# A block-recurrent attention and a bilinear feed-forward in one kernel: the output stage's products in another order, one unit's state copy on ScalarE, one unit's masks apart

## The chip, the cores and the metric

The kernel runs on one core of a Trainium2 chip. The core has five engines with a queue of instructions each. TensorE (PE) multiplies matrices; its weight loads are listed apart as PEld. VectorE (DVE) and ScalarE (ACT) read what PE has written to PSUM, and compute elementwise. GpSimd (POOL) computes elementwise between tiles in SBUF and starts transfers. SyncE (SP) starts transfers. Each engine works through its own queue in order and waits on semaphores for the others. The metric is the time of one execution in microseconds (us) on the device, smaller being better.

## The reference

Four batches of eight heads, 768 positions, 64 values per head. Attention goes through the sequence in blocks of 64: inside a block the scores are masked with a decaying lower triangle, and what came before enters through a 64x64 state per head.

```python
for b in range(nb):
    qb, kb, vb = (q[:, :, sl], k[:, :, sl], v[:, :, sl])
    intra = np.einsum('bhic,bhjc->bhij', qb, kb) * Dmask[None]
    intra = np.einsum('bhij,bhjd->bhid', intra, vb)
    inter = np.einsum('bhid,bhde->bhie', qb * lam_pow[None], kv_state)
    out[:, :, sl] = intra + inter
    kv_state = lam_block * kv_state + np.einsum('bhsd,bhse->bhde', kb_dec, vb)
...
a = x @ w_a          # x: the attention's output, 3072 x 512
b = x @ w_b          # 512 x 1536
return a * b @ w_out # 1536 x 512
```

## The kernel before

**Units and groups.** The 3072 rows are cut into 24 units of 128 rows (a batch has six), and these into seven groups of 4, 2, 4, 4, 4, 4 and 2 units (numbered 0 to 6). The attention works by unit and the feed-forward by group. While the feed-forward of one group runs on PE, pieces of attention for later units are put between its matmuls. Where they go is written out by hand in the table `PLAN`: for each group a list of (slot, piece, unit), and the function `hook(slot)` that the feed-forward calls at fixed points runs the pieces of that slot in the list's order. No planner decides anything at run time: each engine's queue is in the order in which the code issues.

**The pieces.** For unit u, `P` scales q and k by powers of lambda on POOL (L276), starts a transposing transfer on SP (L310) and loads v on POOL's queue (L298). `S` makes the scores: eight 64-row matmuls (L343) into two PSUM banks, then two masking multiplications on DVE into bf16 tiles (L360). `SA` and `SB` are the same cut in two: `SA` issues the matmuls and the first mask, `SB` the second mask (L463). `V` adds a unit to the state in a PSUM bank (L410) and copies it to SBUF: on DVE as one multiplication with a block-diagonal mask (L443), or, for the units in `ACT_COPY`, on ACT as two copies of 64 partitions (L441). `O2` makes the attention outputs of two units: the part from the state (64x64 matmuls) and the part from the masked scores (128x64 matmuls, both L379), which ACT copies to the group's input xT (L402). It then calls `sums` (L560 to L563): for the last unit of a group, four DVE additions that make the tile xs, sums of blocks of xT. It ends with the state matmuls of the second unit (L432), whose copy is made where the other copies are. `Q` is `O2` with one unit's scores beside it.

**The feed-forward** of groups 1 to 6 replaces eight block products with seven (`ffn_seven`). Products run into three kinds of banks, m_q, m_r and m_p (L582), in seven steps per slice of d_ff; ACT copies some banks out (L597: s, s5, u), DVE makes the sums c11 (L616, POOL L619 for some slices), c12 (L627) and c22 (L633) and the product ab (L636), and POOL makes the other half of ab (L629). Three links matter later. The last product of a slice runs into the bank that c22 is read from, so it waits for c22. c12 has two buffers, so the c12 of slice i+2 waits for POOL's ab of slice i. And product n = 3 waits for the copy s5, product n = 7 for the copy u.

**The output stage** of groups 2 to 5 (`out_seven`) does the same with the second matrix: products o_q, o_p, o_r (L693), each of twelve 256-column matmuls in groups of four units, from sums of blocks of ab, called sm, that DVE makes (`add_sums`; L730 makes the set with index 3, L732 the one with index 2). In group 5 an early branch is taken. In groups 2, 3 and 4 the tail issues, in order: o_q from set 1; slots 15 and 16 with the piece `O2`; half of o_r from set 3; o_q from set 2; the DVE addition L787 that reads o_q; the other half of o_r; the DVE addition L789 that reads o_r; the store of o1; slots 17 to 19, among them `G` (POOL waits for the tile xs, so that its next work doesn't start sooner), `P` twice or once, and `S` for the unit after; then a last o_q product into the bank that L787 has read, a copy by ACT (L795), and the store of o2. Stores and transposing transfers stand in the one queue of SP in this order.

**Banks.** PSUM has eight banks. One holds the state. The other seven are given out by `ps_bank`: the one that was used longest ago, among those not held.

Of the kernel before, what the change touches and what calls it, by code (L numbers as in the profile page):

```python
# [22 lines left out]
def _bc(ap, dims):  # L23
# [18 lines left out]
SUM_ON_VEC = {1: (2,), 2: (0, 1, 2, 3, 5), 3: range(6), 4: range(6), 5: (1, 2, 4, 5), 6: (0, 1, 2)}  # L42
O_SEVEN = (2, 3, 4, 5)
O_EARLY = (5,)
ACT_COPY = (4, 10, 12, 13, 14, 16, 17, 18, 20, 21)
FIRST_COPY = (11, 15, 19)
W_ORDER = ("a0", "a1", "b0", "b1", "a2", "b2", "a3", "b3", "a4", "a5", "b4", "b5", "o0", "q4", "k4", "o1", "v4",
           "q5", "k5", "o2", "v5", "o3")
# [14 lines left out]
}  # L63
for _g, _u in ((2, 10), (3, 14), (4, 18)):
    PLAN[_g] += [(11, "V", _u), (13, "Q", (_u, _u + 1, _u + 2)), (14, "V", _u + 2), (14, "S", _u + 3),
                 (16, "O2", (_u + 2, _u + 3)), (18, "S", _u + 4)]
PLAN[2] += [(_s, "W", None) for _s in (3, 3, 3, 4, 4, 4)]


# [1 line left out]
def kernel(  # L71
# [12 lines left out]
    B, H, S, D = q.shape  # L84
# [28 lines left out]
    bank = {"held": set(), "age": [0] * 7, "clock": 0}  # L113
# [155 lines left out]
    U = {}  # L269
# [59 lines left out]
    def score_banks():  # L329
        kq = Banks()  # L330
        kq.ids = []
        for i in range(2):
            kq.append(ps_bank(f"kq{i}", [128, HP, 128], F32))
            kq.ids.append(bank["last"])
        return kq

    def scores(u, kq=None):
        d = U[u]
        kq = kq or score_banks()
        for hp in range(HP):  # L340
            for i in range(2):
                p = slice(64 * i, 64 * i + 64)
                nc.tensor.matmul(kq[i][:, hp, :], lhsT=d["kT"][p, hp, :], rhs=d["qT"][p, hp, :],  # L343
                                 start=True, stop=True, skip_group_check=True)
        return kq

    def masks(u, kq):
        ms = mask(kq)
        U[u]["m"] = lambda i, hp: ms[i][:, hp, :]
# [99 lines left out]
    def piece_SA(u):  # L449
        kq = U[u]["kq"] = scores(u)  # L450
        U[u]["ms"] = [mask_one(kq, 0)]
        return [kq.ids[1]]

    def piece_SB(u):
        ms = U[u]["ms"]
        kq = U[u].pop("kq")
        ms.append(mask_one(kq, 1))
        U[u]["m"] = lambda i, hp: ms[i][:, hp, :]
        return [kq.ids[1]]
# [7 lines left out]
    def piece_V(u):  # L467
        kv_update(u)
        if u % NB < NB - 1:
            kv_copy(u, kv["ps"], "act" if u in ACT_COPY else "dve")  # L470

    xTs = {}

    def pieces_O(us, nxt=()):
        kqs = [score_banks() for u in nxt]
        o_banks(us)
        for u, kq in zip(nxt, kqs):
            scores(u, kq)
        for u in us:
            inter(u)  # L480
        for b in range(2):
            for u in us:
                intra(u, b)
            evac_o(us, b)
        sums(us[-1])
        beside = len(us) == 2 and us[0] >= n0 + 2
        if beside:
            kv_beside(us[1])
        copy = beside and us[1] % NB < NB - 1
        at = 0 if us[1] in FIRST_COPY else 1  # L490
        for n, (u, kq) in enumerate(zip(nxt, kqs)):
            if n == at and copy:
                kv_copy(us[1], kv["ps"])
            masks(u, kq)
        if copy and len(nxt) <= at:
            kv_copy(us[1], kv["ps"], "act" if us[1] in ACT_COPY else "dve")

# [54 lines left out]
    def sums(u):  # L552
        g = next(i for i in range(len(GROUPS)) if g_u0[i] <= u < g_u0[i] + GROUPS[i])
        if g not in S_GROUPS or u != g_u0[g] + GROUPS[g] - 1:
            return
        h = GROUPS[g] * BLK // 2
        x = xTs[u][0]
        t = wst_pool.tile([128, 4, 2, h], BF16, name="xs", tag="wst")
        x11, x12, x21, x22 = (x[:, k:k + 2, c:c + h] for c in (0, h) for k in (0, 2))
        nc.vector.tensor_add(t[:, 0], x22, x21)  # L560
        nc.vector.tensor_sub(t[:, 1], t[:, 0], x11)
        nc.vector.tensor_sub(t[:, 2], x11, x21)
        nc.vector.tensor_sub(t[:, 3], x12, t[:, 1])  # L563
        xs[g] = t
# [110 lines left out]
    def out_seven(u0, n, ab, hook, last_step, early):  # L675
        h, nt, js = n * BLK // 2, n // 2, range(FC // 4)
# [12 lines left out]
        def product(ps, x, w, js, first, ts=range(nt)):  # L689
            for t in ts:  # L690
                for j in js:
                    for c in range(2):
                        nc.tensor.matmul(ps[:, t, :], lhsT=x(j, c)[:, t * BLK:(t + 1) * BLK], rhs=w(j)[:, c, :],  # L693
                                         start=(first and t == 0 and j == js[0] and c == 0), stop=True,
                                         skip_group_check=True)
# [4 lines left out]
        def of_s(i):  # L700
            return lambda j, c: sm[i][j][:, c, :]

        def of_w(k, n):
            return lambda j: wo_block(j, k, n)
# [15 lines left out]
        def add_sums(js, which):  # L720
            for i in which:
                for j in js:
                    x22, x21, x11, x12 = xs4[j]
                    d = [sm[i][j] for i in range(4)]
                    if i == 0:
                        nc.vector.tensor_add(d[0], x22, x21)
                    elif i == 1:
                        nc.vector.tensor_sub(d[1], d[0], x11)
                    elif i == 3:
                        nc.vector.tensor_sub(d[3], x12, d[1])  # L730
                    else:
                        nc.vector.tensor_sub(d[2], x11, x21)  # L732
# [31 lines left out]
        r, rb = bank_of("o_r")  # L764
        product(r, of_s(0), of_t(0), js, True)
        s5 = snap("o_s5", "s5", r, 2)
        if not early:
            hook(FC + 2)
            add_sums(js, (3, 2))
        product(q, of_s(1), of_t(1), js, False)  # L770
        u2 = snap("o_u2", "c12", q, 2)
        if early:
# [9 lines left out]
            return  # L782
        hook(FC + 3)
        hook(FC + 4)
        product(r, of_s(3), of_w(1, 1), js, False, range(nt // 2))
        product(q, of_s(2), of_t(2), js, False)
        nc.vector.tensor_add(o2[:, :, 256:512], s5, q)  # L787
        product(r, of_s(3), of_w(1, 1), js, False, range(nt // 2, nt))
        nc.vector.tensor_add(o1[:, :, 256:512], u2, r)  # L789
        release(rb)  # L790
        put(u0, o1)
# [204 lines left out]
    for g, n in enumerate(GROUPS):  # L996
        if g + 1 < len(GROUPS):
            new_xT(g + 1)
        plan = {}
        for slot, name, us in PLAN.get(g, ()):  # L1000
            plan.setdefault(slot, []).append((name, us))

        def hook(slot, plan=plan):
            for name, us in plan.get(slot, ()):
                if name == "P":
                    prep_k(us)
                    if us in DMA_T:
                        make_vb(us)
                elif name == "QS":
                    make_qs(us, "pool")  # L1010
                elif name == "KS":
                    make_ks(us, "dve")
                    scaled(us)
                elif name == "LS":
                    wait_for(raw[us - 2, "k"])
                    load_x("q", us, nc.sync)
                    load_x("k", us, nc.sync)
                elif name == "L":
                    load_all(us)
                elif name == "TW":  # L1020
                    w_sums(us)
                elif name == "TO":
                    wo_sums(us)
                elif name == "G":
                    gate = singles.tile([1, 1], BF16, name="gate")
                    nc.gpsimd.tensor_copy(gate, xs[max(xs)][0:1, 3, 0, 0:1])
                elif name == "GT":
                    gate = singles.tile([1, 1], BF16, name="gate")
                    nc.gpsimd.tensor_copy(gate, two[max(two)][0:1, 3, 0, 0:1])
                elif name == "W":  # L1030
                    store_kept()
                elif name == "T":
                    piece_T(us)
                elif name == "SA":
                    bank["held"].update(piece_SA(us))
                elif name == "SB":
                    bank["held"].difference_update(piece_SB(us))
                elif name == "S":
                    piece_S(us)
                elif name == "V":  # L1040
                    piece_V(us)
                elif name == "O":
                    pieces_O((us,))
                elif name == "O2":
                    pieces_O(us)
                else:
                    pieces_O(us[:2], us[2:])

        if g in S_GROUPS:
            ffn_seven(g, g_u0[g], n, gx.pop(g), hook, g + 1 == len(GROUPS))  # L1050
        else:
            ffn(g_u0[g], n, gx.pop(g), hook, g == 0)
# [29 lines left out]
```

## Time and profile before

| | us |
|---|---|
| median of 9 runs | 218.79 |
| lowest, highest | 218.12, 221.62 |
| the profiled execution | 218.8 |
| its span in the profile | 217.1 |
| PE busy | 208.7 (96% of the span) |
| DVE busy | 175.3 (81%) |
| ACT busy | 106.6 (49%) |
| POOL busy | 124.7 (57%) |
| share of PE in the chain that ended last | 91% |

Busy times are the unions of the engine's instructions. The profiled execution took 1.7 us more than its span; that part lies before the first and behind the last recorded instruction. The granted clock of TensorE is at full speed in all slices. A timeline row gives start, length, engine, line, operation, tiles and count; a row of several matmuls ends, by the model for matmul ends, about 0.16 us after the next row may start, so the start of the next row is what counts. In square brackets stands how long the engine was idle before the row, and what released it.

### The profile page before, as it was taken

What the parts mean: (1) busy time and instruction counts of PE and PEld (TensorE: products, weight loads), DVE (VectorE), ACT (ScalarE), POOL (GpSimd) and SP (SyncE); (2) the same over time, 40 slices, a digit from 0 to 9 for tenths busy, and PEclk for the clock granted to TensorE, in tenths of its full rate; (3) what the DMA queues carried; (4) which work ended last, traced back from release to release, by engine and by line L of the source; (5) the groups of instructions that cost most, each with busy time, mean ns of one, the idle gap of its engine ahead of it and who ended that gap; (6) DMA issues with size and microseconds to landing.
All of it is one profiled execution on the core that took longest, in us unless ns stands there. A gap on an engine that the chain in (4) does not pass through costs nothing.

```text
span 217.1 us, 5765 instructions
## 1 busy us (share of the span) xinstructions
PE 208.7 (96%) x2323; PEld 161.9 (75%) x2331; DVE 175.3 (81%) x322; ACT 106.6 (49%) x195; POOL 124.7 (57%) x143
## 2 busy tenths in 40 slices
PE   7699999999899999999999999999999999999994
PEld 2376444555796688878888987888987888889973
DVE  0892899777878988999789999689999588996860
ACT  2586224256751565446465535555545556344522
POOL 5879659974679199820999310999310736300330
PEclk9999999999999999999999999999999999999999
DMA  4999999999999999990499990699900750002302
GB/s 125 301 177 188 196 230 215 224 217 188 132 196 171 159 168 264 242 226 13 126 190 190 227 145 3 144 174 230 138 0 3 151 118 0 3 2 78 118 3 97
DMA packets 86766, 31.31 MB, mean 144 GB/s; under 512 B 74068, under 2 KB 83156, under 8 KB 86740
## 3 DMA queue, kind: packets, MB, share of 16 engines
q1 hardware_dynamic: 53748, 20.39, 47.6%
q0 software_dynamic: 32704, 10.49, 43.0%
q8 instruction: 18, 0.29, 0.6%
q10 hardware_dynamic: 288, 0.07, 0.1%
q14 instruction: 8, 0.07, 0.1%
HBM read 28.32 MB, written 6.29 MB: 159 GB/s over the span
## 4 chain that ended last, share of the span: by engine, by line
PE 91%; DMA 3%; DVE 1%; SPq 1%; issue 1%; ACT 1%; ACTq 0%
PE m_q L582 24%; PE m_r L582 12%; PE op L819 10%; PE o_q L693 10%; PE m_p L582 6%; PE o_r L693 5%; PE o_ps L379 5%; PE b_ps L505 5%; PE a_ps L505 5%; PE kq L343 3%; DMA k<-in_k_dram 3%; PE o_p L693 2%; PE kvd L410 1%; SPq L229 1%; PE tps L321 1%
## 5 line engine op out<-in xcount | busy, mean ns | idle before, releaser
L629 POOL TENSOR_TENSOR ab<-c,c 128x512 bf16<-128x512 bf16 x30 | 34.9, 1168 | 33.5 <-DVE c L627 33.2
L582 PEld LDWEIGHTS <-tw 128*128 128x128 bf16 x576 | 48.7, 98 | 6.8 <-issue 1.3
L582 PE MATMUL m_q<-xs,tw 128*128 128x256 bf16 (+1 forms) x288 | 36.1, 255 | 0.1
L360 DVE TENSOR_TENSOR m<-kq,lotri 128x512 bf16<-128x512 f32 x41 | 25.8, 681 | 2.1 <-PE kq L343 2.1
L582 PEld LDWEIGHTS <-wa_sb 128*128 128x128 bf16 x288 | 24.7, 98 | 2.6
L597 ACT COPY s<-m_q 128x512 f32<-128x512 f32 x30 | 17.6, 588 | 17.8 <-PE m_q L582 17.6
L636 DVE TENSOR_TENSOR ab<-c,m_q 128x512 bf16<-128x512 f32 x30 | 20.5, 684 | 6.0 <-PE m_q L582 4.2
L627 DVE TENSOR_TENSOR c<-u,m_r 128x512 f32<-128x512 f32 x30 | 20.4, 681 | 3.7 <-ACT u L597 3.7
L298 POOL DMA_DIRECT2D vb<-in_v_dram x24 | 22.3, 932 | 1.3 <-DMA wo_sb<-in_moe_w_out_dram 1.2
L819 PE MATMUL op<-wo_sb,ab 128*128 128x512 bf16 (+2 forms) x114 | 22.1, 335 | 0.4 <-issue 0.2
L616 DVE TENSOR_TENSOR c<-s,m_p 128x512 bf16<-128x512 f32 x25 | 17.1, 685 | 6.7 <-PE m_p L582 5.8
L597 ACT COPY s<-m_r 128x512 f32<-128x512 f32 x30 | 17.7, 590 | 8.9 <-PE m_r L582 8.9
L597 ACT COPY u<-m_q 128x512 f32<-128x512 f32 x30 | 17.7, 591 | 7.2 <-PE m_q L582 5.9
L633 DVE TENSOR_TENSOR c<-s,m_q 128x512 f32<-128x512 f32 x30 | 20.5, 685 | 0.4
L693 PEld LDWEIGHTS <-sm 128*128 128x128 bf16 x192 | 17.5, 98 | 3.6 <-DVE sm L732 0.4
L276 POOL TENSOR_TENSOR qk<-qf,lp_q 128x512 bf16<-128x512 f32 x18 | 18.9, 1050 | 1.4 <-DMA qf<-in_q_dram 1.4
L582 PE MATMUL m_q<-xT,tw 128*128 128x256 bf16 (+1 forms) x144 | 18.1, 255 | 0.9 <-DVE c L633 0.9
L402 ACT CAST xT<-o_ps 128x512 bf16<-128x512 f32 x22 | 11.9, 588 | 12.9 <-PE o_ps L379 12.6
L582 PE MATMUL m_r<-xs,tw 128*128 128x256 bf16 (+1 forms) x144 | 18.1, 255 | 0.0
L582 PE MATMUL m_r<-xs,wb_sb 128*128 128x256 bf16 (+1 forms) x144 | 18.1, 255 | 0.0
L582 PE MATMUL m_q<-xT,wa_sb 128*128 128x256 bf16 (+1 forms) x144 | 18.1, 255 | 0.0
L582 PE MATMUL m_p<-xT,wa_sb 128*128 128x256 bf16 (+1 forms) x144 | 18.1, 255 | 0.0
(120 smaller groups left out, 362.3 us busy)
## 6 DMA issues: line engine op xcount, KB each, us to landing
out_dram<-o_two SPq DMA_DIRECT2D x8, 512.0 KB, 3.4
qf<-in_q_dram SPq DMA_DIRECT2D x14, 256.0 KB, 5.8
kf<-in_k_dram SPq DMA_DIRECT2D x14, 256.0 KB, 6.1
vb<-in_v_dram POOLq DMA_DIRECT2D x24, 128.0 KB, 5.9
wa_sb<-in_moe_w_a_dram POOLq DMA_DIRECT2D x6, 256.0 KB, 6.1
wb_sb<-in_moe_w_b_dram POOLq DMA_DIRECT2D x6, 256.0 KB, 7.5
wo_sb<-in_moe_w_out_dram POOLq DMA_DIRECT2D x6, 256.0 KB, 8.2
out_dram<-o_kept SPq DMA_DIRECT2D x6, 256.0 KB, 5.1
```

Source lines behind the costliest of these rows:

```text
L276: eng_of(eng).tensor_mul(dst.rearrange("p (c b) d -> p b c d", b=2), x[:].rearrange("p (b c) d -> p b c d", b=2), lp.rearrange("p (b c) o ...
L298: nc.gpsimd.dma_start(out=vb, in_=vr[b, nb])
L360: nc.vector.tensor_mul(m, kq[i], lotri_bc)
L505: nc.tensor.matmul(ps[:, lo:hi], lhsT=w_sb[:, s, f * 128:(f + 1) * 128], rhs=xT[:, s, lo:hi], start=(s == 0), stop=(s == KS - 1), skip_gro ...
L582: nc.tensor.matmul(ps[:, f, :], lhsT=w(k, f), rhs=x[:, k, :], start=(first and f == 0 and k == 0), stop=True, skip_group_check=True)
L597: nc.scalar.copy(t, ps)
L627: nc.vector.tensor_add(c12, d["u2"], d["r"])
L629: nc.gpsimd.tensor_mul(ab[:, nf * i:nf * i + nf, 0:h], d["c11"], c12)
L633: nc.vector.tensor_add(d["c22"], d["s5"], d["q"])
L636: nc.vector.tensor_mul(ab[:, nf * i:nf * i + nf, h:2 * h], d["c22"], d["q"])
L693: nc.tensor.matmul(ps[:, t, :], lhsT=x(j, c)[:, t * BLK:(t + 1) * BLK], rhs=w(j)[:, c, :], start=(first and t == 0 and j == js[0] and c == ...
L819: nc.tensor.matmul(op[:, lo:hi], lhsT=ab[:, f, t * 128:(t + 1) * 128], rhs=wo_sb[:, f, lo:hi], start=(f == 0), stop=(f == FC - 1))
```

## The change

Three things are changed, all in the order of issue or in the engine that does a piece. The arithmetic is the same, and so is the number of matmuls.

1. In the output stage of groups 2, 3 and 4, the piece `S` of slot 18 is cut in two: its score matmuls (`SK`) go to slot 16, ahead of the attention outputs, and its two masks (`SM`) to slot 17, behind `G` and `P`. Between `SK` and `SM` its two banks are held. The piece `O2` is called without its four sums (`OD`); they are issued later, behind L787. The two halves of o_r's product are joined and come behind o_q from set 2, and `add_sums` makes set 2 before set 3.
2. In group 1, the state copy of unit 6 moves from DVE to ACT.
3. In group 1, unit 7's scores and first mask are issued in slot 1 and its second mask in slot 2; the outputs of units 6 and 7 move from slot 4 to slot 5, between the scores and the masks of unit 8.

```diff
-ACT_COPY = (4, 10, 12, 13, 14, 16, 17, 18, 20, 21)
+ACT_COPY = (4, 6, 10, 12, 13, 14, 16, 17, 18, 20, 21)
...
-    1: [(0, "V", 6), (1, "S", 7), (4, "O2", (6, 7)), (4, "P", 10), (5, "S", 8),
+    1: [(0, "V", 6), (1, "SA", 7), (2, "SB", 7), (4, "P", 10), (5, "SK", 8), (5, "O2", (6, 7)), (5, "SM", 8),
         (6, "V", 8), (6, "P", 11), (7, "S", 9), (12, "O2", (8, 9))],
...
-                 (16, "O2", (_u + 2, _u + 3)), (18, "S", _u + 4)]
+                 (16, "SK", _u + 4), (16, "OD", (_u + 2, _u + 3)), (17, "SM", _u + 4)]
...
+    def piece_SK(u):
+        kq = U[u]["kq"] = scores(u)
+        return kq.ids
+
+    def piece_SM(u):
+        kq = U[u].pop("kq")
+        masks(u, kq)
+        return kq.ids
...
-    def pieces_O(us, nxt=()):
+    def pieces_O(us, nxt=(), defer=False):
...
-        sums(us[-1])
+        if defer:
+            late.append(us[-1])
+        else:
+            sums(us[-1])
...
-            add_sums(js, (3, 2))
+            add_sums(js, (2, 3))
...
-        product(r, of_s(3), of_w(1, 1), js, False, range(nt // 2))
         product(q, of_s(2), of_t(2), js, False)
         nc.vector.tensor_add(o2[:, :, 256:512], s5, q)
-        product(r, of_s(3), of_w(1, 1), js, False, range(nt // 2, nt))
+        while late:
+            sums(late.pop())
+        product(r, of_s(3), of_w(1, 1), js, False)
...
+                elif name == "SK":
+                    bank["held"].update(piece_SK(us))
+                elif name == "SM":
+                    bank["held"].difference_update(piece_SM(us))
+                elif name == "OD":
+                    pieces_O(us, defer=True)
```

More of the change, by code (lines that the diff above doesn't have):

```diff
@@ L470, in piece_V @@
             kv_copy(u, kv["ps"], "act" if u in ACT_COPY else "dve")
-    xTs = {}
-    def pieces_O(us, nxt=()):
+    xTs, late = {}, []
+    def pieces_O(us, nxt=(), defer=False):
         kqs = [score_banks() for u in nxt]
```

## The prediction, made before the changed kernel ran

> **What bounds the kernel now.** I read the engines' busy times and the summary of the chain that ended last first, then that chain inside group 1, then the timelines of PE and DVE in the output stage of group 3.
>
> ```profile
> PE 208.7 (96%) x2323; PEld 161.9 (75%) x2331; DVE 175.3 (81%) x322; ACT 106.6 (49%) x195; POOL 124.7 (57%) x143
> ...
> PE 91%; DMA 3%; DVE 1%; SPq 1%; issue 1%; ACT 1%; ACTq 0%
> ```
>
> PE sets the time nearly everywhere, so a change pays only where it shortens PE's own work or a wait of PE. The chain shows one stretch in group 1 where DVE leads:
>
> ```profile
> 55.93 0.57 PE m_r L582 x8
> ...
> 57.12 1.27 DVE m L360 x2
> 58.39 0.59 DVE c L627
> 58.99 0.61 DVE c L633
> 59.60 0.04 issue
> 59.64 0.61 PE m_q L582 x8
> ```
>
> The product at 59.64 waits for c22 (L633), and c22 stands in DVE's queue behind unit 6's state copy (56.52), unit 7's two masks (57.12) and c12. PE issued the product before at 58.11 and needs 0.45 for it, so it was ready at 58.56: 1.08 lost.
>
> PE, output stage of group 3:
>
> ```profile
> 130.59 1.49 PE L693 MATMUL o_q<-two,sm 128*128 128x256 bf16 x12
> 132.01 0.42 PE L379 MATMUL o_ps<-qkT,st 64*64 64x128 bf16 x16
> 132.36 0.64 PE L379 MATMUL o_ps<-m,vb 128*64 128x128 bf16 x16
> 132.93 0.83 PE L693 MATMUL o_r<-wo_sb,sm 128*128 128x256 bf16 x6
> 133.59 1.59 PE L693 MATMUL o_q<-two,sm 128*128 128x256 bf16 x12
> 135.02 0.82 PE L693 MATMUL o_r<-wo_sb,sm 128*128 128x256 bf16 x6
> 135.77 0.40 PE L343 MATMUL kq<-qkT 64*128 64x128 bf16 x8
> 136.19 1.47 PE L693 MATMUL o_q<-two,ab 128*128 128x256 bf16 x12
> 137.50 0.60 PE L582 MATMUL m_q<-xT,wa_sb 128*128 128x256 bf16 x4
> ```
>
> Read from start to start, twelve matmuls take 1.31 undisturbed (the last product) and six take 0.66 (132.93 to 133.59). Three rows are longer. DVE in the same stretch says why:
>
> ```profile
> 132.99 1.09 DVE L732 TENSOR_TENSOR sm<-ab 128x512 bf16<-128x512 bf16 x3
> 134.00 0.41 DVE L560 TENSOR_TENSOR xs<-xT 128x512 bf16<-128x512 bf16 x1
> ...
> 135.46 0.68 DVE L787 TENSOR_TENSOR o_two<-o_s,o_q 128x512 f32<-128x512 f32 x1
> 136.06 0.68 DVE L789 TENSOR_TENSOR o_two<-o_u,o_r 128x512 f32<-128x512 f32 x1
> ```
>
> The second o_q takes 1.43: its set 2 is finished only at 134.08. The second half of o_r takes 0.75: 0.09 is the switch from full matmuls to 64-row ones. The scores take 0.42 where 0.33 is usual (130.26 to 130.59): the last o_q must wait until L787 has read the bank, at 136.14.
>
> **The output stage, groups 2 to 4.** No matmul is added or removed. In group 3 the new order costs: o_q from set 1 with the switch 1.42, the scores 0.33, the state part of the outputs 0.35, the mask part 0.57 (all as above), then o_q, o_r and o_q at 1.31 each, 6.60 from 130.59 instead of 6.91: 0.31 saved. (Between scores and outputs nothing more is paid than the 0.33: at 127.25 and 127.58 of the trace the same sequence stands.) Group 2, 98.65 to 105.47, has 6.82 and comes to 1.42 + 0.33 + 0.93 + 3.93 = 6.61: 0.21. Group 4, 162.75 to 169.77, has 7.02 and comes to 1.41 + 0.33 + 1.04 + 3.93 = 6.71: 0.31. Together 0.83.
>
> Does a new wait take this back? In group 3, on the trace's clock: set 2 is now made first and ends at 133.08, and o_q from it begins at 133.26. Set 3 ends at 134.08, o_r begins at 134.57. L787 can start when o_q has ended, 134.83, and has read the bank at 135.5; the last o_q begins at 135.88. The scores come 3.7 earlier, and need their transposed q and k: unit 18's transfer starts at 121.13 and lands 6.7 later, at 127.8, for scores at 132.0. For units 14 and 22 it lands at 97.2 and 158.1, for scores at 100.1 and 164.2.
>
> What comes later is DVE. It idles from 134.08 to 134.83, then L787 until 135.43, the four sums 1.46 until 136.89, L789, and the two masks from 137.49 to 138.69, instead of 137.85. The next group's c11 is the next in that queue. It waits for m_p, which ends about 0.31 earlier than before, near 138.76: just covered (before, DVE idled 1.15 there). The second product of the group needs the first sum only, ready at 135.85. With the masks gone late, their banks are wanted by the next slice's m_r, at 140.86 before. L789's bank is wanted at 139.4. Both have a microsecond or more. So I book 0 here; without the cover each 0.1 of DVE would cost PE at most 0.1, through c12 and c22.
>
> [...] Two banks are now held through the outputs, beside o_q and o_r. Following the rule of `ps_bank`, the outputs get the banks of the second and third mask ahead of them in DVE's queue (in group 2: masks from 97.51 in steps of 0.61, the third read by 99.4; the outputs start at 100.4). By the row the price is 0; if pressure bit, with the banks of a mask not begun, it would be those 0.6 per mask, 1.8 over three groups. I take the row.
>
> POOL is moved too: `G` waits for the sums. Its copy goes from 103.58 to about 104.9 (+1.3) in group 2, and from 135.67 to 136.8 (+1.1) in group 3. Behind it wait the scalings, the v loads, SP's transposing transfers, the loads behind these, the store of o2, and POOL's ab. The one that meets PE: c12 of slice 4 waits for ab of slice 2. In group 3 that ab runs 117.75 to 118.9 and c12 starts at 120.80; after, 120.3 against 120.5. In group 4, 151.0 against 153.07 becomes 152.1 against 152.4. Margins of 0.2 and 0.3, so 0, but thin.
>
> **Group 1.** The copy leaves DVE (0.60 from start to start) and becomes two ACT copies. The rows of these have 0.37 each, 0.39 apart, so 0.78; the trace doesn't show another ACT copy right behind, so 0.64 (overlapped as the others are by 0.12 to 0.15) to 0.78. I take 0.78. [...] c22 doesn't depend on that much: DVE makes m0 at 56.52, c12 at 57.15 (u ends at 57.10), c22 from 57.80 to 58.48. PE, with product n = 7 at 57.15 and four more of 0.45, is ready at 58.94. No wait is left: 59.64 becomes 58.94, 0.70 gained.
>
> Most of it is lost again. The outputs of 6 and 7 now come behind unit 8's scores: one switch less (0.1), scores at 62.16, outputs at 62.5 (the second bank, of m_p, is read by c11 until 62.51: 0.08). The last state matmul starts at 63.37, and L443 for unit 7 follows 0.24 later, at 63.61. It now stands ahead of unit 8's masks, so the first starts at 64.21; before, at 64.32. From there DVE works without a gap in both orders: two masks, L636, c12, c22, the state copy of 8, two masks of 9, until 69.20. The outputs of 8 and 9 wait for the last mask: their last four matmuls started at 69.25. So PE arrives 0.6 early and waits; **0.11** is left. Group 2 follows with DVE full and PE full, both 0.11 earlier.
>
> **The sum**: 0.83 + 0.11 = 0.94. The profiled execution was 218.8 with a span of 217.1; the span becomes 216.2 and the time 217.9. The median of the runs, 218.79, is the same as the profiled one: **217.85**.
>
> **Rivals.**
> - A, *the gain of group 1 stays*: DVE has less behind it than I think, and PE keeps 0.6 to 0.8. For it: DVE idles 0.24 and 0.37 near 62 and 63 before. Against: its gapless row to 69.20. 218.79 - 0.83 - 0.7 = 217.25.
> - B, *slower*: POOL's late start becomes the wait. Place: c12 of slice 4 in groups 3 and 4. It decides from 0.2 and 0.3 beyond the delay worked out, and from there costs one for one. Were POOL one microsecond later still, because unit 18's k is loaded behind two delayed transposing transfers on SP (its scaling starts at 114.82, the load was issued at 108.21, and such loads take 6.1), it would cost 0.8 + 0.7: 219.35. Against: POOL found that k without a wait, and load and scaling are delayed alike.
> - C, *the waits only move*: the two short waits per output stage return at the head of the next group, where DVE has lost its 1.15 of slack, and only the switch (0.09 each) and little of group 1 stay: 218.45.
>
> **How the numbers follow.** Mine 0.55, with its own range 217.5 to 218.2; A 0.18, B 0.13, C 0.14. A measurement of this kernel tells about 0.2%, 0.44, from no change: faster below 218.35. Mine nearly wholly, A, and a quarter of C are faster, 0.75; the rest of C and a little of mine the same, 0.12; B slower, 0.13. The range 217.1 to 218.6 holds mine, most of A and most of C; B is left out.
>
> **What would show it.** In each output stage: o_q, o_r, o_q back to back at 1.31, and 6.6 to 6.7 from the second o_q to the next group. In group 1: no idle time ahead of the product that waits for c22, L443 of unit 7 near 63.6, and a new PE wait of about half a microsecond ahead of the outputs of 8 and 9. I am wrong if c12 of slice 4 waits for POOL, if c11 at a group's head waits for DVE's masks by more than 0.1, or if the outputs of 8 and 9 start over 0.3 earlier.

## The result and the profile after

The changed kernel takes 217.43 us in the median of 9 runs (217.17 to 217.58), beside 218.38 for the kernel before in the same measurement. The ratio is 0.9956, 95% interval 0.9942 to 0.9969: 0.44% faster. The prediction was 217.85, with a range of 217.1 to 218.6. The profiled execution took 217.47 with a span of 215.8; that of the kernel before took 218.8 with a span of 217.1. So the medians differ by 0.95 and the two profiles by 1.33: the profiled execution of the kernel before lies 0.4 above the median measured here, that of the kernel after on its median. What is read from one execution each is good for a mechanism and its size, but 0.4 between two executions of one program is within what is seen: the nine of the changed kernel alone lie 0.41 apart.

The page of the kernel after, busy times and the chain that ended last:

```profile
PE 209.1 (97%) x2323; PEld 162.7 (75%) x2331; DVE 175.4 (81%) x321; ACT 107.4 (50%) x197; POOL 124.2 (58%) x143
...
PE 89%; DMA 3%; ACT 2%; DVE 2%; issue 2%; SPq 1%
```

PE's 2323 matmuls are the same work; it does them in a span 1.3 us shorter. The timeline of PE in group 3's output stage of the kernel after (start, length, engine, line, operation, tiles, shape, count):

```profile
130.10 1.48 PE L705 MATMUL o_q<-two,sm 128*128 128x256 bf16 x12
131.52 0.40 PE L343 MATMUL kq<-qkT 64*128 64x128 bf16 x8
131.85 0.42 PE L379 MATMUL o_ps<-qkT,st 64*64 64x128 bf16 x16
132.19 0.64 PE L379 MATMUL o_ps<-m,vb 128*64 128x128 bf16 x16
132.76 1.48 PE L705 MATMUL o_q<-two,sm 128*128 128x256 bf16 x12
134.09 1.47 PE L705 MATMUL o_r<-wo_sb,sm 128*128 128x256 bf16 x12
135.40 1.47 PE L705 MATMUL o_q<-two,ab 128*128 128x256 bf16 x12
136.71 0.60 PE L594 MATMUL m_q<-xT,wa_sb 128*128 128x256 bf16 x4
```

L705 is the old L693, L594 the old L582; the other new numbers are L628 for L616, L639 for L627, L645 for L633, L648 for L636, L742 and L744 for L730 and L732, L798 for L787, L808 for L795, L572 for L560. From start to start the three products behind the outputs now take 1.33, 1.31 and 1.31, and the stage 6.61 from 130.10 to 136.71, against 6.91 before. DVE in the same stretch:

```profile
131.50 1.08 DVE L744 TENSOR_TENSOR sm<-ab 128x512 bf16<-128x512 bf16 x3
132.51 1.09 DVE L742 TENSOR_TENSOR sm<-ab,sm 128x512 bf16<-128x512 bf16 x3
134.34 0.69 DVE L798 TENSOR_TENSOR o_two<-o_s,o_q 128x512 f32<-128x512 f32 x1 [0.75 <-ACT xT L402]
```

Set 2 is ready at 132.58, before PE wants it at 132.76, and L798 has read its bank 0.4 us before the last o_q begins at 135.40.

Group 1, PE of the kernel after. The first row is product n = 3, the second the product that used to wait for c22:

```profile
56.05 0.61 PE L594 MATMUL m_r<-xs,wb_sb 128*128 128x128 bf16 x8 [0.22 <-ACT s L609]
58.81 0.61 PE L594 MATMUL m_q<-xT,tw 128*128 128x128 bf16 x8
...
68.15 0.73 PE L379 MATMUL o_ps<-m,vb 128*64 128x128 bf16 x12
69.06 0.30 PE L379 MATMUL o_ps<-m,vb 128*64 128x128 bf16 x4 [0.18 <-DVE m L360]
```

And DVE there:

```profile
63.54 0.69 DVE L443 TENSOR_TENSOR st<-kvd,bdiag 128x512 bf16<-128x512 f32 x1 [1.09 <-PE kvd L432]
64.15 1.28 DVE L360 TENSOR_TENSOR m<-kq,lotri 128x512 bf16<-128x512 f32 x2
...
67.73 1.27 DVE L360 TENSOR_TENSOR m<-kq,lotri 128x512 bf16<-128x512 f32 x2
```

The wait ahead of the product is gone; the new wait at the outputs of units 8 and 9 is there: the twelve matmuls at 68.15 take 0.91 to the next start, of which some 0.55 is the wait for the last mask.

The table sets out where the span went. A group's length runs from its first feed-forward product to that of the next group; groups 5 and 6 are alike to 0.01.

| us | before | after | gained |
|---|---|---|---|
| group 1 begins | 53.43 | 53.32 | 0.11 |
| group 1 | 19.64 | 19.56 | 0.08 |
| group 2 | 32.40 | 32.10 | 0.30 |
| group 3 | 32.02 | 31.72 | 0.30 |
| group 4 | 32.27 | 31.73 | 0.54 |

### The profile page after: what moved, and what is told of

Read it like the earlier page. It is cut to its first block, busy times and chain, and to the rows that moved or that the text cites. A ratio compares the mean times of both kernels' runs of the same rounds, so it can differ in the third digit from the quotient of the medians.

```text
span 215.8 us, 5766 instructions
## 1 busy us (share of the span) xinstructions
PE 209.1 (97%) x2323; PEld 162.7 (75%) x2331; DVE 175.4 (81%) x321; ACT 107.4 (50%) x197; POOL 124.2 (58%) x143
## 3 DMA queue, kind: packets, MB, share of 16 engines
q1 hardware_dynamic: 53748, 20.39, 47.4%
## 4 chain that ended last, share of the span: by engine, by line
PE 89%; DMA 3%; ACT 2%; DVE 2%; issue 2%; SPq 1%
PE m_q L594 23%; PE m_r L594 12%; PE o_q L705 9%; PE op L832 8%; PE m_p L594 6%; PE o_r L705 5%; PE b_ps L517 5%; PE o_ps L379 5%; PE a_ps L517 5%; DMA k<-in_k_dram 3%; PE kq L343 3%; PE o_p L705 2%; SPq L229 1%; PE kvd L410 1%; DVE m L360 1%
## 5 line engine op out<-in xcount | busy, mean ns | idle before, releaser
L594 PEld LDWEIGHTS <-tw 128*128 128x128 bf16 x576 | 48.7, 98 | 5.5 <-issue 0.2
L594 PE MATMUL m_q<-xs,tw 128*128 128x256 bf16 (+1 forms) x288 | 36.1, 255 | 0.0
L594 PEld LDWEIGHTS <-wa_sb 128*128 128x128 bf16 x288 | 24.7, 98 | 2.6
L360 DVE TENSOR_TENSOR m<-kq,lotri 128x512 bf16<-128x512 f32 x39 | 24.6, 681 | 1.6 <-PE kq L343 1.6
L648 DVE TENSOR_TENSOR ab<-c,m_q 128x512 bf16<-128x512 f32 x30 | 20.5, 684 | 5.8 <-PE m_q L594 4.0
L639 DVE TENSOR_TENSOR c<-u,m_r 128x512 f32<-128x512 f32 x30 | 20.4, 681 | 2.7 <-ACT u L609 2.7
L645 DVE TENSOR_TENSOR c<-s,m_q 128x512 f32<-128x512 f32 x30 | 20.5, 685 | 0.4
L628 DVE TENSOR_TENSOR c<-s,m_p 128x512 bf16<-128x512 f32 x25 | 17.1, 685 | 4.5 <-PE m_p L594 3.6
L1039 POOL COPY gate<-xs 1x1 bf16<-1x1 bf16 x3 | 0.5, 176 | 34.3 <-DVE xs L575 34.3
L705 PEld LDWEIGHTS <-sm 128*128 128x128 bf16 x192 | 17.9, 98 | 2.8 <-DVE sm L738 0.2
L594 PE MATMUL m_r<-xs,wb_sb 128*128 128x256 bf16 (+1 forms) x144 | 18.0, 254 | 0.2 <-ACT s L609 0.2
L594 PE MATMUL m_r<-xs,tw 128*128 128x256 bf16 (+1 forms) x144 | 18.1, 255 | 0.0
L594 PE MATMUL m_q<-xT,tw 128*128 128x256 bf16 (+1 forms) x144 | 18.1, 255 | 0.0
L594 PE MATMUL m_q<-xT,wa_sb 128*128 128x256 bf16 (+1 forms) x144 | 18.1, 255 | 0.0
```

The lines of the kernel that those rows point to most:

```text
L360: nc.vector.tensor_mul(m, kq[i], lotri_bc)
L594: nc.tensor.matmul(ps[:, f, :], lhsT=w(k, f), rhs=x[:, k, :], start=(first and f == 0 and k == 0), stop=True, skip_group_check=True)
L639: nc.vector.tensor_add(c12, d["u2"], d["r"])
L645: nc.vector.tensor_add(d["c22"], d["s5"], d["q"])
L648: nc.vector.tensor_mul(ab[:, nf * i:nf * i + nf, h:2 * h], d["c22"], d["q"])
```

## The experiments

Theory: the output stage earns about 0.8, through two short waits per stage and one switch; group 1 earns 0.1, because what DVE gets back early it loses at L443 of unit 7. Rivals: group 1's gain stays (A), POOL's late gate bites (B), the waits only move (C). Ratios are to the kernel before, measured beside each kernel; their intervals are 0.2 to 0.7% wide, so the lengths of groups in the profiles carry the fine comparisons. All edits but those marked are against the kernel after.

### The two parts apart

The output stage alone:

```diff
-ACT_COPY = (4, 6, 10, 12, ...
+ACT_COPY = (4, 10, 12, ...
-    1: [(0, "V", 6), (1, "SA", 7), (2, "SB", 7), (4, "P", 10), (5, "SK", 8), (5, "O2", (6, 7)), (5, "SM", 8),
+    1: [(0, "V", 6), (1, "S", 7), (4, "O2", (6, 7)), (4, "P", 10), (5, "S", 8),
```

> The output stage's reordering alone, with group 1 as before. My theory: it holds 0.83 of the 0.94, so 0.83 off a before of about 218.4, ratio 0.9962; the three stages from the second o_q to the next group take 6.6, 6.6 and 6.7. Rival C (the waits only move to the next group's head): 0.3 off, ratio 0.9987. If group 1 gave most of the gain: under 0.3 off.

Measured: 217.31, ratio 0.9961 (0.9934 to 0.9989). Groups 2 to 4 last 32.20, 31.72 and 31.74, so 1.03 less than before. Group 1 lasts 20.05 in this profile, 0.41 more than before though its code is the same, and the profiled execution, 218.03, is 0.72 above the median. So the same code of group 1 took 0.41 longer in this execution than in that of the kernel before; what lies behind it comes below.

Group 1's part alone, with the output stage as before (tail order, sums and `add_sums` restored):

> Group 1's part alone (unit 6's copy on ScalarE, unit 7's masks apart, the outputs of 6 and 7 behind unit 8's scores), output stages as before. My theory: the product that waits for c22 comes 0.7 earlier, but only 0.11 of it is left at the head of group 2, because L443 of unit 7 heads a gapless row on VectorE: ratio 0.9995. Rival A: 0.7 is left, ratio 0.9968.

Measured: 218.38, ratio 0.9989 (0.9974 to 1.0003), group 1 19.57, group 2 32.31, groups 3 and 4 as before. The 0.09 that group 2 gains lies at the first product of o_r, whose weights wait 0.15 for DVE's sums, where they wait 0.25 in the kernel before: DVE gets there 0.1 earlier. Rival A falls: its 0.9968 is outside the interval. The gain is the output stage's.

### What takes group 1's gain away

The outputs of units 6 and 7 put back to slot 4; copy and masks stay as changed:

```diff
-    1: [..., (2, "SB", 7), (4, "P", 10), (5, "SK", 8), (5, "O2", (6, 7)), (5, "SM", 8),
+    1: [..., (2, "SB", 7), (4, "O2", (6, 7)), (4, "P", 10), (5, "S", 8),
```

> The changed kernel, with the outputs of units 6 and 7 put back to slot 4 and unit 8's scores and masks together in slot 5, as before; one switch more on TensorE. My theory: the state copy of unit 7 starts near 61.7 instead of 63.5, the masks of unit 8 near 63.5 instead of 64.15, and group 2 starts about 0.6 earlier than in the changed kernel: 1.55 off before, ratio 0.9929. If the later place of the outputs is what brings group 1's gain: 0.1 slower than the changed kernel, ratio 0.996.

Measured: 216.80, ratio 0.9907 (0.9874 to 0.9940), faster than both kernels. Group 1 lasts 18.93. DVE, then PE, of this kernel:

```profile
61.55 0.69 DVE L443 TENSOR_TENSOR st<-kvd,bdiag 128x512 bf16<-128x512 f32 x1 [0.25 <-PE kvd L432]
...
66.91 1.28 DVE L360 TENSOR_TENSOR m<-kq,lotri 128x512 bf16<-128x512 f32 x2
```

```profile
67.84 0.71 PE L379 MATMUL o_ps<-m,vb 128*64 128x128 bf16 x16
```

L443 comes 1.99 earlier than in the kernel after, the masks of unit 9 0.82 earlier (0.18 of each is an earlier start of the group), and the sixteen mask matmuls run in one row without a wait.

Leaving the outputs at slot 5 and giving ACT unit 7's state copy too, so that L443 leaves DVE's row:

```diff
-ACT_COPY = (4, 6, 10, ...
+ACT_COPY = (4, 6, 7, 10, ...
```

> The changed kernel, with unit 7's state copy on ScalarE too. My theory: VectorE's row no longer starts with that copy, the masks of unit 8 start near 62.5, unit 8's state matmuls wait 0.2 for ScalarE, and TensorE doesn't wait for the masks of 9: group 2 starts 0.4 earlier than in the changed kernel, 1.35 off before, ratio 0.9938. If VectorE's row is not what holds the outputs of 8 and 9: 0.2 slower than the changed kernel for the wait on ScalarE, ratio 0.9965.

Measured: 217.01, ratio 0.9925 (0.9900 to 0.9950), group 1 19.06. Two different ways of freeing DVE's row ahead of the last masks bring 0.5 and 0.6 us: the row was the limit, as the prediction said.

A third variant: the outputs at slot 4, and unit 6's state copy on DVE, but behind c22 (`VM` is the state matmuls alone, `VC` the copy):

```diff
-    1: [(0, "V", 6), (1, "SA", 7), (2, "SB", 7), ...
+    1: [(0, "VM", 6), (1, "SA", 7), (2, "VC", 6), (2, "SB", 7), (4, "O2", (6, 7)), (4, "P", 10), (5, "S", 8),
```

> The kernel with unit 8's scores put back behind the outputs of units 6 and 7, and besides that unit 6's state copy taken from ScalarE and put on VectorE behind the first slice's c22. My theory: what is left of a stall in group 1's first slices is ScalarE's (the product m_r of slice 3 waits 0.22 for the s copy that stands behind the two state copies), so it goes, the first n=4 product stays where it is, and VectorE, which idles 0.25 ahead of L443 of unit 7, takes the 0.6 us copy partly in that gap: group 1 becomes 0.2 to 0.3 us shorter than the 18.93 us with ScalarE's copy, ratio to the kernel before 0.9895. Rival: the copy's 0.6 us on VectorE pushes L443 of unit 7 and the masks behind it by 0.35 and what ScalarE saves is eaten: 18.93 or longer, ratio 0.991 to 0.992.

Measured: 216.56, ratio 0.9914 (0.9893 to 0.9935). Group 1 lasts 18.57, 0.36 less than with ACT's copy, where 0.2 to 0.3 was expected; but group 2 lasts 32.68 instead of 32.27 and takes it back. So the ratio is the one that the rival named, for a reason which neither theory had. DVE and POOL at the end of group 1 in this kernel:

```profile
69.16 1.18 DVE L572 TENSOR_TENSOR xs<-xT 128x512 bf16<-128x512 bf16 x1 [0.62 <-ACT xT L402]
```

```profile
69.02 1.03 POOL L276 TENSOR_TENSOR qk<-qf,lp_q 128x512 bf16<-128x512 f32 x1
```

The sum L572 takes 0.42 in the kernel after, 0.77 where it meets this scaling halfway (the outputs at slot 4), and 1.18 here, where it begins 0.14 behind it and lasts until 0.3 after it. So the sum that came earlier met POOL's scaling and was slowed; DVE reached group 2's first c22 late, and PE waited 0.43 for it at 76.85.

### Each step of the output stage

The order of the two sets put back:

```diff
-            add_sums(js, (2, 3))
+            add_sums(js, (3, 2))
```

> The changed kernel, with set 3 of the sums made ahead of set 2 again. My theory: o_q from set 2 waits in every output stage, 0.34, 0.45 and 0.42 by the changed kernel's trace: 1.2 slower than the changed kernel, about 0.3 over before, ratio 1.001. If VectorE's sums are hidden: as the changed kernel, 0.9956.

Measured: 218.68, ratio 1.001 (1.000 to 1.002). Groups 2 to 4 lose 0.34, 0.46 and 0.44 to the kernel after, and the row tells why:

```profile
133.31 1.72 PE L705 MATMUL o_q<-two,sm 128*128 128x256 bf16 x12 [0.15 <-DVE sm L744]
```

With the halves of o_r joined behind it, o_q has nothing in front of it to cover its set. This one swap is what makes the rest of the new order worth having.

The four sums right behind the outputs, ahead of L798, as before:

```diff
-                    pieces_O(us, defer=True)
+                    pieces_O(us)
```

> The changed kernel, with the four sums for the next group issued right behind the outputs again, ahead of L787. My theory: L787 ends at 103.85, 135.65 and 167.37 on the changed kernel's clock, the last o_q of each stage waits for it 0.23, 0.30 and 0.29: 0.8 slower than the changed kernel, ratio 0.9993. GpSimd's gate comes 1.4 earlier. Rival C (a wait saved there returns at the next group's head anyway): no slower than the changed kernel, 0.9956.

Measured: 219.10, ratio 1.0033 (1.0022 to 1.0044), where I had expected 0.9993. DVE, then PE:

```profile
134.07 0.42 DVE L572 TENSOR_TENSOR xs<-xT 128x512 bf16<-128x512 bf16 x1 [0.17 <-ACT xT L402]
...
135.54 0.68 DVE L798 TENSOR_TENSOR o_two<-o_s,o_q 128x512 f32<-128x512 f32 x1
```

```profile
136.27 1.47 PE L705 MATMUL o_q<-two,ab 128*128 128x256 bf16 x12 [0.41 <-DVE o_two L798]
```

The last o_q waits for L798, and the groups lose 0.43, 0.57 and 0.67 to the kernel after. I had left out that the sums cannot start before ACT's copy to xT ends, so L798 came 0.1 to 0.3 later than reckoned. Some 0.24 of the last number is the pause of ACT below.

The scores behind the outputs again, all else as after:

```diff
-                 (16, "SK", _u + 4), (16, "OD", (_u + 2, _u + 3)), (17, "SM", _u + 4)]
+                 (16, "OD", (_u + 2, _u + 3)), (18, "S", _u + 4)]
```

> The changed kernel, with the scores and masks of the unit after back in slot 18, behind o_r; the sums still late. My theory: one switch more per stage, o_r with the scores 0.09 longer: 0.3 slower than the changed kernel, ratio 0.9968. If the place of the scores saved nothing: 0.9956. If the held banks cost something: faster than the changed kernel.

Measured: 217.76, ratio 0.9971 (0.9961 to 0.9982). The groups lose 0.10, 0.11 and 0.11: the price of one more switch between full matmuls and 64-row ones, measured by itself. PE in this kernel:

```profile
134.03 1.47 PE L705 MATMUL o_r<-wo_sb,sm 128*128 128x256 bf16 x12
135.44 0.40 PE L343 MATMUL kq<-qkT 64*128 64x128 bf16 x8
```

o_r's twelve take 1.41 to the next start, where they take 1.31 with another full product behind them.

So the words of the change, "scores right ahead of attention outputs", name the part worth 0.3 in all; order of the sets and place of the sums are worth 1.2 and 1.4, each taken alone from the finished order (without that pause).

### POOL's margin (rival B)

Five memsets of an unused 128x128 tile on POOL behind each `G`, extra work only:

```diff
                     nc.gpsimd.tensor_copy(gate, xs[max(xs)][0:1, 3, 0, 0:1])
+                    for _ in range(5):
+                        nc.gpsimd.memset(idle_pool, 0.0)
```

> The changed kernel, with five small memsets on GpSimd behind each of its three gates, d in all (0.65 to 1.5, by the 0.52 of the 512-column memsets). My theory: the changed kernel stands with no margin for VectorE and 0.33 for TensorE, so c12 of slice 4 comes d later in groups 3 and 4 and TensorE loses d - 0.4 and d - 0.33: for d = 1.0, 1.3 slower than the changed kernel, ratio 1.0015; the price of rival B. If GpSimd is hidden well: 0.9956.

Measured: 219.08, ratio 1.0032 (1.0021 to 1.0043). POOL's first scaling began 1.32 behind the gate instead of 0.14, so the delay was 1.18. PE of this kernel, groups 3 and 4 (its lines are one further on than those of the kernel after):

```profile
122.58 0.60 PE L595 MATMUL m_q<-xT,tw 128*128 128x256 bf16 x4 [0.51 <-DVE c L646]
...
154.95 0.60 PE L595 MATMUL m_q<-xT,tw 128*128 128x256 bf16 x4 [0.44 <-DVE c L646]
```

and the cause on DVE:

```profile
121.24 0.69 DVE L640 TENSOR_TENSOR c<-u,m_r 128x512 f32<-128x512 f32 x1 [0.99 <-POOL ab L642]
```

The mechanism of rival B is real and stands where I put it: c12 of slice 4 waits for POOL's ab, and c22 and the product behind it. Groups 3 and 4 lose 0.67 and 0.65. So the delay that PE stands is 1.18 less these, 0.51 and 0.53, beyond what the change itself uses up.

### The pause of ScalarE in group 4

Group 4 gained 0.54 where 0.31 was predicted. The timeline of ACT at its head, kernel before:

```profile
138.65 0.61 ACT L597 COPY s<-m_r 128x512 f32<-128x512 f32 x1
139.79 0.58 ACT L597 COPY u<-m_q 128x512 f32<-128x512 f32 x1 [0.53 <-PE m_q L582]
```

The semaphore record ahead of the u copy ends at 139.47, and the copy starts 0.32 later, where 0.04 to 0.07 is usual. PE's next product waits for it and loses 0.24. It is the gap between the 190th and the 191st record of ACT's queue, semaphores counted and the first one numbered 0, and it shows there also in the kernels with group 1's part alone and with the early sums, whatever they do in between. The test: one more ACT instruction ahead of it, at the end of group 2, with nothing waiting for it. First in the kernel before, then in the kernel after:

```diff
                     nc.gpsimd.tensor_copy(gate, xs[max(xs)][0:1, 3, 0, 0:1])
+                    if g == 2:
+                        nc.scalar.copy(tick, lotri[0:1, 0:1])
```

> The kernel before with one more ScalarE instruction, a copy of 1x1, in ScalarE's idle time at the end of group 2's output stage; nothing waits for it. It tests where the 0.32 us pause of ScalarE at the head of group 4 belongs, which cost TensorE 0.24 us in the kernel before and is not seen there in the kernel after. Theory: the pause belongs to a place in ScalarE's own stream of instructions (between its 190th and 191st record), so that one instruction more ahead of it moves it to the instruction before, where ScalarE waits for TensorE anyway: the record ahead of the u copy of the first slice takes 0.06 instead of 0.32, group 4 lasts 32.03 us instead of 32.27, the span 216.86 instead of 217.1, ratio 0.9989. Rival: the pause belongs to the place in the work (or to the moment, a transfer under way): it stays, 32.27, ratio 1.0000.

> The kernel after with the same extra 1x1 copy by ScalarE at the end of group 2's output stage. Theory of a place in ScalarE's stream: the 190th record is now the wait ahead of the first slice's s copy of m_r in group 4, the pause of 0.32 us becomes visible there and TensorE waits for it as it did in the kernel before: group 4 lasts 31.95 us instead of 31.73, ratio to the kernel before 0.9967 instead of 0.9956. Rival, that the output stage's new order took the pause away by its timing: 31.73, ratio 0.9956.

ACT of the kernel before with the extra copy (its lines, too, are one further on):

```profile
137.70 0.60 ACT L598 COPY s<-m_r 128x512 f32<-128x512 f32 x1
138.55 0.59 ACT L598 COPY u<-m_q 128x512 f32<-128x512 f32 x1 [0.25 <-PE m_q L583]
```

PE of the kernel after with the extra copy:

```profile
138.36 0.60 PE L595 MATMUL m_q<-xs,tw 128*128 128x256 bf16 x4
139.08 0.60 PE L595 MATMUL m_r<-xs,wb_sb 128*128 128x256 bf16 x4
```

The product n = 3 starts 0.72 behind the one before it, where 0.49 is usual. Both group lengths came out within 0.02: group 4 lasts 32.03 in the one (32.27 without the copy) and 31.96 in the other (31.73 without). The pause sits at a place in ACT's own queue, and the change escaped it because it shifted that queue by a record, not because of its order. So 0.24 of the gain in the profile is an accident. What ACT does in the pause no run here shows. (In the four traces that have it, one packet of 8192 bytes of the instruction queue starts 1.4 to 2.9 us after it; whether the two belong together stays open.)

But the first of the two had a ratio of 0.9943 (0.9923 to 0.9963), 218.40 against 217.18, five times what the pause is worth; in its profile group 1 lasted 19.02 instead of 19.64. The second had 0.9949 (0.9932 to 0.9966) where 0.9967 was expected, although its profile has group 1 at 19.57, as without the copy, and no group shorter: where its median gained, I can't say.

### The late k, and what it did to group 1

The tile for the extra copy moved every tile laid out behind it by 32 bytes per partition. Read again with this in mind, the kernel before shows on DVE, ahead of the row that the prediction quoted:

```profile
55.91 0.69 DVE L276 TENSOR_TENSOR qk<-qkf,lp_k 128x512 bf16<-128x512 f32 x1 [0.79 <-DMA qkf<-in_k_dram]
56.52 0.68 DVE L443 TENSOR_TENSOR st<-kvd,bdiag 128x512 bf16<-128x512 f32 x1
```

DVE stood still for 0.79 until unit 9's k had landed, and c22 stands behind that. The kernel after has a wait of the same kind,

```profile
55.32 0.69 DVE L276 TENSOR_TENSOR qk<-qkf,lp_k 128x512 bf16<-128x512 f32 x1 [0.96 <-DMA qkf<-in_k_dram]
```

but there the row behind it is short enough that PE doesn't feel it. In the kernel before with the extra copy, and so with the shift, k's load was issued 1.9 us sooner (48.63 instead of 50.48) and DVE never waited for k. The output stage alone, with the shift and not one instruction added, moved or removed:

```diff
-    lotri = singles.tile([128, 128], BF16, name="lotri")
+    lotri = singles.tile([128, 144], BF16, name="lotri")[:, 0:128]
```

> The kernel with the output stage's part alone, same instructions in the same order, and one thing besides: the tile lotri is given 144 columns in place of 128 and its first 128 are used, so that every tile laid out behind it (the buffers of q, k, v, of the outputs and of the products) stands 32 bytes further on in each partition, at addresses that are multiples of 64 bytes where they were 32 beyond one. The two kernels with the extra 1x1 copy had the same shift, and in both the hardware queue's packets took 41.4 and 42.3% of the span against 46.9 to 48.5% in the eleven other profiles; unit 9's k landed in time for VectorE and group 1 of the kernel before lasted 19.02 us instead of 19.64. Theory of the address: it does it alone; packets near 42%, no wait of VectorE ahead of L276, group 1 at 19.0 us instead of 20.05, span 215.1 to 215.3, ratio 0.991. That would also say that the change's own part in group 1, which lasts 19.57 with the shift and 19.56 without it, gains only by hiding a late k and costs 0.55 where k is in time. Rival, the copy of 1x1 or the chip of that day did it: packets near 47%, group 1 at 20.05, span 216.3, ratio 0.9961.

Measured: 217.00, ratio 0.9911 (0.9881 to 0.9941), span 215.4. Time of the hardware queue's packets as a share of the span, kernel before, then this kernel (queue, packets, MB, share):

```profile
q1 hardware_dynamic: 53748, 20.39, 47.6%
```

```profile
q1 hardware_dynamic: 53748, 20.39, 41.0%
```

and DVE of this kernel:

```profile
55.09 0.68 DVE L276 TENSOR_TENSOR qk<-qkf,lp_k 128x512 bf16<-128x512 f32 x1
```

The same packets take a seventh less time, k is there, and group 1 lasts 18.56 instead of 20.05. The addresses do it. It isn't the moving as such: the unused tile of the run on POOL's margin moves the same buffers by 256 bytes, which leaves them 32 beyond a multiple of 64, and the packets take 47.1% there. Moved by 32, the buffers of q, k, v and of the outputs stand at multiples of 256 bytes and not of 64 only; which of the two counts, one shift can't tell.

The table cuts group 1 at the product that waits for c22 in the first slice:

| us | to the product | from it to group 2 |
|---|---|---|
| before | 6.21 | 13.43 |
| after | 5.49 | 14.07 |
| output stage alone | 6.61 | 13.44 |
| outputs 6 and 7 at slot 4 | 5.49 | 13.44 |
| same, unit 6's copy late on DVE | 5.13 | 13.44 |
| before, with the copy and the shift | 5.59 | 13.44 |
| after, with the copy and the shift | 5.49 | 14.08 |
| output stage alone, with the shift | 5.12 | 13.44 |

5.12 is PE without any wait. The right column is the same 13.44 in every kernel that has the outputs of 6 and 7 at slot 4, and 0.64 more in the two that have them at slot 5. That price is paid whether k is late or not, as long as L443 of unit 7 stays on DVE; with unit 7's copy on ACT, the column is 13.57. The left column depends on when k lands: 5.12 to 6.61 with the old order (5.59 with k in time, where the scaling L277 ahead of it takes 1.31 beside one of POOL's, instead of 0.69), 5.49 with the new one in all three kernels, two waits for ACT (0.29 and 0.08) being the rest. So the change's part in group 1 makes the kernel indifferent to a k as late as seen here, and gains 0.1 to 0.5 in group 1 where k is late; where k is in time, it costs 0.55 to 1.01 by these profiles. The ratios say the same less sharply: without the shift 0.9956 with that part and 0.9961 without; with the shift 0.9949 with it, of which 0.0011 is the pause, and 0.9911 without, with intervals that overlap.

## Why the prediction was right, point by point

**The output stage, 0.83.** Right, in its mechanism and size. The stages were to last 6.61, 6.60 and 6.71; they last 6.61, 6.61 and 6.73, 0.80 less than before. The second o_q, the joined o_r and the last o_q run at 1.31 to 1.33, and the swap and the place of the scores each cost what the step says of them when taken back; the place of the sums cost more, 1.4 instead of 0.8.

**No new wait in the output stage.** Right. The masks are done before the next group's c11, which starts when m_p is there: 0.71 behind m_p's first matmul in groups 3 and 4 (105.86 to 106.57, 137.58 to 138.29), as in the kernel before. The price of the two held banks was taken as 0 and not as the 1.8 of outputs that wait for masks not begun, and the outputs follow the scores in 0.33 (131.52 to 131.85) while the two are held.

**POOL's gate, 0 with thin margins.** The 0 was right: the gate comes at 104.85 and 136.63 as worked out, and PE loses nothing. The margins of 0.2 and 0.3 were set for c12's start; in group 4 of the kernel after that c12 does wait for POOL and comes 0.1 late, which I had named as a sign of being wrong. It costs nothing, because its c22 had slack of its own behind it, 0.33 there, and PE stands 0.5 more delay. For PE the margins were too small, because I followed the chain to c12 and not on to the product.

**ACT's two copies, 0.78.** The first starts at 54.62, and the copy behind them at 55.41: 0.79. So the second copy is not overlapped by the first, and the upper end of the range, 0.64 to 0.78, was the right one to take. Product n = 3 starts 0.62 behind the scores ahead of it (55.43 to 56.05), where 0.33 is usual: a wait of 0.29 for ACT.

**Group 1, 0.70 gained and 0.59 lost.** Measured 0.72 and 0.64, net 0.08 instead of 0.11: L443 of unit 7 at 63.54, as predicted for 63.61 on a clock that runs 0.11 earlier. The sizes hold, but the reading of what PE waited for in the kernel before was incomplete. I named unit 6's copy, the masks and c12 as the row ahead of c22, and overlooked that DVE had stood idle for 0.79 at its head. The removed copy (0.60) did shorten that row, so the sum came out; that the row was long enough to matter was mostly due to a late transfer.

**The sum, 0.94.** 0.95 between the medians, 1.33 between the two spans. Of the 0.39 by which the spans differ more, 0.24 is ACT's pause, which no step foresaw and which has nothing to do with the new order; 0.11 is an earlier start of group 1, whose code ahead of it is the same (over the fourteen profiles it lies between 53.06 and 53.86); 0.09 is the shorter wait of o_r's first product in group 2, which group 1's part brings; the stages and group 1 gave 0.03 less each. That the medians fall on the sum so closely is therefore partly luck: the profiled execution that I worked from lies 0.4 above the median measured beside the changed kernel. The time is 0.42 below the number and inside the range.

**The rivals.** A fell with group 1's part alone. C fell with the lengths of the groups: nothing of the stages' gain comes back at the next group's head. B has the right place and a threshold that this change doesn't reach.

## What to carry to other kernels

Follow a wait back to the idle time at the head of the row, not to the longest piece in it: what is shown as waiting for VectorE can be a transfer that is late. When two halves of a product covered the making of an operand, joining them asks for another order of the operands too; here the joining without it loses everything (1.001 instead of 0.9956). And before giving a reordering credit for a few tenths of a microsecond, shift the queue by one dummy instruction and the tiles by some bytes: in this kernel the first moved 0.24 us and the second about 1, as much as the edit.

## What the runs showed of the hardware that I had not expected

- **A pause at a fixed place of ScalarE's queue.** 0.32 us between its 190th and 191st record, in four kernels with different work there, moved by one extra instruction in two tests. In the kernel after, ACT waits for a product of PE at that place, with a gap of 0.19 ahead of the 191st record, and no pause shows. At the 65th record of the kernel after, a semaphore record is followed by a gap of 0.34 us too, but the copy behind it starts 0.48 behind the copy before, the usual pace, so that this is a second such pause is not shown.
- **With the tiles at another place, the transfers took less time.** With all later tiles 32 bytes further on, from 32 beyond a multiple of 64 bytes to a multiple, the hardware queue's 53748 packets take 41.0 to 42.3% of the span in three kernels, against 46.9 to 48.5% in the eleven others, one of which has the same buffers 256 bytes further on.
- **A bf16 addition on VectorE that started beside a GpSimd multiplication ended 0.3 after it.** 0.42 alone, 0.77 and 1.18 with the multiplication of bf16 from f32 beside it, in two profiles. In the kernel before, two additions of L726 take 0.75 at 94.11, with GpSimd at rest, and 1.34 at 125.01, beside its product ab; the first of these ends at 126.01, 0.28 behind the product.
- The fastest kernels here, the outputs at slot 4 (0.9907), the output stage alone with the shift (0.9911) and unit 6's copy late on VectorE (0.9914), can't be told apart; the first or the last with the shift was not tried.
